# Attention, rational MLP and soft mixture of experts in one launch: accumulating DMAs started later, a conversion split between engines, more buffers for expert weights and a new table of priorities

## The chip, the cores and the metric

One core of a Trainium2 chip runs the whole program in one launch. The metric is the device time of that launch in microseconds (us). The core has TensorE (PE), VectorE (DVE), ScalarE (ACT), GpSimd (POOL) and SyncE (SP, which only issues DMAs here); 16 DMA engines are shared by all queues.

## The reference, cut to what matters

The three stages follow each other; `x` has 4608 rows of 512. Eight batches of 576 rows make up the 4608.

```python
k_p = k.reshape(B, H, Sp, pool, D).mean(axis=3)      # pool = 8, Sp = 72
v_p = v.reshape(B, H, Sp, pool, D).mean(axis=3)
attn = softmax(scale * q @ k_p.T);  x = attn @ v_p   # 8 heads of 64, to (4608, 512)

h = x @ w_in                                         # (4608, 2048)
P = a[0] + a[1]*h + a[2]*h*h + a[3]*h*h*h
Q = 1.0 + abs(b[0])*abs(h) + abs(b[1])*h*h
x = (P / (Q + 1e-6)) @ w_out                         # (4608, 512)

logits = x @ phi                                     # 32 slots: 8 experts of 4
d = softmax(logits, axis=0);  slot_input = d.T @ x
slot_out[e] = relu(slot_input[e] @ w1[e]) @ w2[e]    # each expert: 512 -> 1024 -> 512
out = softmax(logits, axis=1) @ slot_out
```

`w_in` and `w_out` arrive as 64-bit floats; all the rest is 32-bit.

## The kernel before, in words

The rows are cut into 36 tiles of 128, and the tiles into nine **runs** of four (`NR` = 9). `w_out` is never multiplied with the rows: it is folded into the router (`wpt`) and applied to the 32 slots at the end, so only the activation `A` of the MLP is kept.

- **Attention** (`attention(t)`, lines 410 to 490), one tile: scores `sc`, maximum, exponential, sum, normalisation, transposes `pt`, products `av`, and the split of the result into a rounded part `xh` and a rest `xl`. The tiles of run 0 come first; those of run r+1 are computed while run r is in its dense part.
- **Dense** (`dense(r, p)`), eight pairs of 128 columns a run: 24 products a pair into the buffer `h` (lines 558 to 560, two `h` buffers of two PSUM banks), then ACT (`s`, `a`, `u`), POOL (lines 577, 583, 585) and DVE (lines 580, 592, 594, 596) compute the rational function into `A`; `lg` (line 606) are the logits, line 617 transposes `A` into `G`. A new pair's products wait until line 580 has read the `h` that they overwrite.
- **Routing** (`routing(r)`) after a run: the maximum of the slots, the exponential `L`, its transposes `ptq` and `ptr`, a copy `en`, 128 products `pss` that sum `A` by slots, and their addition to the running sum `Sacc` (line 709).
- **Weights** (`win`, `wout`, `words`): each of 32 blocks of 512 KB is loaded as two 32-bit words per number and put together: one ACT operation on the high word (line 501), three DVE operations (lines 502, 504, 506). `win` then splits into `wh` (ACT 515, POOL 516), `wout` makes a column of `wpt` (products `wot`, `pw`).
- **Pooled keys and values**: batch 0 is reduced on DVE, the others by DMAs that add in DRAM (`summed`): one plain copy on SP, then seven accumulating DMAs on the POOL queue, each of which waits for the one before to land. Batch 1 has its own pair (`kr`, `vr`, 144 KB each DMA), batches 2 to 7 share one (`ksum`, `vsum`, 864 KB each).
- **Experts and tail**: `experts()` loads 8 blocks of `w_out` and 64 of `w1` and `w2`, 512 KB each, into whatever buffer has become free; `tail()` finishes the slots (`stp`, `slin`, `pi`), multiplies with `w1` (`l`) and `w2` (`lo`), and writes 18 blocks of the output.
- 120 idle products (line 327, each two records in the trace) fill PE's gaps before the first dense product.

The order on every engine is made when the program is built, by `Plan.run()`: a list scheduler with a duration for every operation. It takes the operation that could start first and, among equals, the one with the smallest key. A row of constants (`HEAD`, `FIRST`, `RUN`, `K_...`) gives the keys; they name times but only rank. Some operations carry an alternative on another engine (`alt`), allowed in run 0 and in the last run from pair `EITHER` on. Engines then execute that order strictly.

Of the kernel before, what the change touches and what calls it, by code (L numbers as in the profile page):

```python
# [10 lines left out]
I32 = mybir.dt.int32  # L11
AF = mybir.ActivationFunctionType
# [6 lines left out]
SP = 72  # L19
NT = B * S  # L20
DM = 512
# [9 lines left out]
HEAD, FIRST, RUN = 27.2, 101.2, 69.79  # L31
ATT, ATO = 18.86, -18.84
# [5 lines left out]
FINE, EITHER = 2, 6  # L38
LGN, LGL = 1, 7
RW, GD, AD = 2, 6, 0  # L40
A1, A1S = 23.71, 10.22
K_AS, K_A1, K_W, K_UW, K_LN, K_EX, K_U, K_A, K_LG, K_T, K_GT = 2.1, 7.21, -0.59, 8.21, 10.79, 0.89, 16, 0.1, 5.04, 27.99, 27.09
K_S, K_S1, K_S2, AXR = -14.78, 117.23, 23.77, 3
K_R, K_P1, K_P, K_IN, K_OUT, K_AT = 12.5, 13.81, 61.38, -40, -14.54, 1.58
# [78 lines left out]
class Task:  # L123
    __slots__ = ("alts", "key", "deps", "outs", "bufs", "n", "end", "start", "idx", "nbytes", "ready", "kind", "name")


class Plan:
# [46 lines left out]
    def run(self):  # L174
# [6 lines left out]
        for t in self.tasks:  # L181
            t.ready = 0.0
# [6 lines left out]
        while left:  # L189
# [16 lines left out]
            for t in live:  # L206
                s0 = t.ready
                if best and round(max(s0, min(free[a[0]] for a in t.alts)), 3) > best[0][0]:
                    continue
# [14 lines left out]
                for i, (e, d, fn, p) in enumerate(t.alts):  # L224
# [5 lines left out]
                    k = (round(s, 3), t.key, s + d, t.idx)  # L230
# [35 lines left out]
def soft_moe_kernel(ctx: ExitStack, tc: tile.TileContext, qT, kT, vP, kS, vS, kR, vR, w_in, w_out, ab, phi, w1, w2, sel, pick, out):  # L266
# [37 lines left out]
    vp = [fixed([SP, DM], f"vp{i}", np_=4) for i in range(2)]  # L304
# [11 lines left out]
    idle = buf("lg", [128, 128], "idle")  # L316
    lgb = buf("lg", [128, 2, 130], "lg", np_=2)
# [8 lines left out]
    for _ in range(FILL):  # L326
        op("PE", 0.22, lambda: p_.matmul(idle.t, ident, ident, start=True, stop=True), [idb], [idle], 1e6)
# [6 lines left out]
    run_len = lambda r: FIRST if r == 0 else RUN  # L334
# [24 lines left out]
    def summed(src, shape, name, key, step):  # L359

        d = fixed(shape, name, pool_=dr)
        n = 4 * shape[0] * shape[1]
        op("SP", 0.06, lambda: nc.sync.dma_start(out=d.t, in_=src[0]), [], [d], key, nbytes=2 * n)
        for w in range(1, 8):
            op("POOL", 1.0, lambda w=w: g_.dma_start(out=d.t, in_=src[w], accum_op=ALU.add, max_dma_last_dim=4 * shape[1]), [], [d], key + step * w, nbytes=3 * n)
        return d
# [3 lines left out]
    def pooling(b):  # L370
        need = att_key(first_tile[b])
        kb, vb = kp[b % 2], vp[b % 2]
        if b > 0:
            g, i, n = (0, 0, 1) if b == 1 else (1, b - 2, B - 2)
# [8 lines left out]
            op("SP", 0.06, lambda: nc.sync.dma_start(out=vb.t, in_=at_(1, SP)), [pooled[g][1]], [vb], key, nbytes=SP * 2048)  # L383
# [12 lines left out]
        for i in range(4):  # L396
# [4 lines left out]
            op("DVE", 1.2, lambda t=t, o=o, i=i: v_.tensor_reduce(out=o.t[:, 128 * i : 128 * i + 128], in_=t.t, axis=AX.X, op=ALU.add),  # L401
               [], [t, (o, i)], key, alt=[("POOL", 2.5, lambda t=t, o=o, i=i: tree(t.t, o.t[:, 128 * i : 128 * i + 128]), True)] if E0 & 8 else ())
# [3 lines left out]
    def attention(t):  # L406
# [87 lines left out]
    def words(src, t, key):  # L494
# [152 lines left out]
    def routing(r):  # L647
# [39 lines left out]
        for q in range(4):  # L687
# [11 lines left out]
            if q == 0:  # L699
                pssed[r] = P.tasks[-1]  # L700
# [314 lines left out]
```

## Time and profile before

| | |
|---|---|
| time, median of 3 runs | 868.07 us (867.98 to 869.91) |
| profiled execution | 867.88 us, of it 866.1 us span from first to last instruction |
| PE, DVE, ACT, POOL busy | 775.3, 665.6, 568.6, 500.6 us |
| first dense product of run 0, of run 1 | at 61.1 and 185.1 us |
| maximum of the slots (line 660) of run 1, 7, 8 | at 289.4, 706.8 and 766.1 us |
| mean granted clock of TensorE | 0.945 of full speed |

Two kinds of rows are read below: busy times by stretch, with the granted clock (1.00 is 2.4 GHz, 0.50 is 1.2 GHz) and the busy share of the DMA engines; and single waits, where the text behind `<-` names what ended them.

### The profile page before, as it was taken

To read this page: it belongs to the slowest core of one execution; us is meant where nothing else is said; L and a number is where in the kernel's file an instruction comes from. 1 tells how busy PE (TensorE), PEld (TensorE's weight loads), DVE (VectorE), ACT (ScalarE), POOL (GpSimd) and SP (SyncE) were. 2 spreads that over 40 slices of the span, in tenths; PEclk is the share of its full clock that TensorE was granted. 3 is DMA by queue.
4 is the path that set the end of the run, shared out by engine and by line. 5 is a ranking of instruction groups with operands and counts; after the bars stand their busy time and mean duration, and the time that the engine had idled before them with its cause. 6 is when DMAs were issued, how large, how long until landed. Compare 5 with 4: busy or idle time off the path is not lost.

```text
span 866.1 us, 15758 instructions
## 1 busy us (share of the span) xinstructions
PE 775.3 (90%) x6250; PEld 567.0 (65%) x6250; DVE 665.6 (77%) x977; ACT 568.6 (66%) x960; POOL 500.6 (58%) x304
## 2 busy tenths in 40 slices
PE   9889876999899999999999999999999988559992
PEld 9767655676777677677777768767767756324320
DVE  5757989774899898889998988989888888861011
ACT  2356856657678778968868877877896773721032
POOL 2524546146778767867858858876886875800000
PEclk9959968989999999999999999999999999969997
DMA  9997367972400000000000000000000643549959
GB/s 325 257 318 220 112 169 187 181 163 49 93 25 20 20 26 20 20 25 13 20 20 13 26 17 20 15 12 26 13 14 26 218 123 90 195 135 411 409 209 350
DMA packets 34709, 99.70 MB, mean 115 GB/s; under 512 B 4052, under 2 KB 5204, under 8 KB 34572
## 3 DMA queue, kind: packets, MB, share of 16 engines
q1 hardware_dynamic: 31724, 84.25, 27.9%
q0 software_dynamic: 2912, 14.45, 9.3%
q8 instruction: 49, 0.80, 0.4%
q14 instruction: 24, 0.20, 0.1%
HBM read 85.05 MB, written 30.15 MB: 133 GB/s over the span
## 4 chain that ended last, share of the span: by engine, by line
PE 61%; DVE 13%; ACT 12%; POOL 6%; DMA 4%; issue 2%; SPq 0%; ACTq 0%; DVEq 0%; POOLq 0%
PE h L558 13%; PE h L560 11%; PE h L559 11%; POOL a L577 5%; PE av L483 4%; DVE a L580 3%; PE sc L426 3%; PE pt L472 3%; PE lo L873 3%; PE lg L606 3%; ACT s L572 3%; DMA G<-in_w_out 2%; PE pw L537 2%; PE pss L694 2%; PE l L844 2%
## 5 line engine op out<-in xcount | busy, mean ns | idle before, releaser
L558 PE MATMUL h<-xh,wh 128*128 128x512 f32 x576 | 246.8, 428 | 19.0 <-DVE a L580 10.7
L560 PE MATMUL h<-xh,wh 128*128 128x512 f32 x576 | 230.9, 401 | 2.4 <-POOL wh L516 2.3
L559 PE MATMUL h<-xl,wh 128*128 128x512 f32 x576 | 230.3, 400 | 0.0
L577 POOL TENSOR_TENSOR a<-a,s 128x1024 f32<-128x1024 f32 (+1 forms) x66 | 154.3, 2338 | 86.7 <-ACT s L572 56.4
L585 POOL TENSOR_TENSOR u<-u,s 128x1024 f32<-128x1024 f32 (+1 forms) x72 | 168.2, 2338 | 5.6
L558 PEld LDWEIGHTS h<-xh,wh 128*128 128x128 f32 x576 | 110.6, 192 | 56.4 <-DVE a L580 15.5
L560 PEld LDWEIGHTS h<-xh,wh 128*128 128x128 f32 x576 | 110.5, 192 | 29.4 <-POOL wh L516 3.2
L559 PEld LDWEIGHTS h<-xl,wh 128*128 128x128 f32 x576 | 111.0, 193 | 19.5 <-DVE xl L488 0.4
L592 DVE SCALAR_TENSOR_TENSOR u<-u,r 128x512 f32<-128x512 f32 x144 | 96.5, 673 | 31.3 <-ACT r L591 30.9
L580 DVE SCALAR_TENSOR_TENSOR a<-h,abt,a 128x1024 f32<-128x1024 f32 (+1 forms) x74 | 92.6, 1251 | 33.2 <-POOL a L577 29.0
L574 ACT ACTIVATE a<-h,abt 128x1024 f32<-128x1024 f32 (+1 forms) x71 | 84.9, 1196 | 39.0 <-PE h L560 39.0
L591 ACT ACTIVATE r<-s 128x512 f32<-128x512 f32 x144 | 86.8, 604 | 30.6 <-DVE a L596 28.5
L594 DVE SCALAR_TENSOR_TENSOR r<-a,abt,r 128x512 f32<-128x512 f32 x144 | 106.0, 739 | 0.0
L583 POOL TENSOR_SCALAR s<-u,gb 128x1024 f32<-128x1024 f32 (+1 forms) x72 | 88.6, 1230 | 25.5 <-DVE a L577 14.2
L596 DVE SCALAR_TENSOR_TENSOR a<-u,r 128x512 f32<-128x512 f32 x144 | 97.5, 680 | 3.0
L588 ACT ACTIVATE s<-u,cc 128x1024 f32<-128x1024 f32 (+1 forms) x74 | 83.6, 1129 | 8.6 <-POOL u L585 6.2
L572 ACT ACTIVATE s<-h 128x1024 f32<-128x1024 f32 (+1 forms) x74 | 73.8, 998 | 21.4 <-PE h L560 18.4
L617 DVE STREAM_TRANSPOSE G<-a 128x1024 f32<-128x1024 f32 x64 | 79.0, 1237 | 1.0
L463 POOL TENSOR_TENSOR at<-at,st 128x576 f32<-128x576 f32 x35 | 40.6, 1161 | 66.8 <-PE av L483 26.5
L576 ACT ACTIVATE u<-h 128x1024 f32<-128x1024 f32 (+1 forms) x74 | 74.2, 1002 | 3.5 <-PE h L560 2.1
L475 ACT ACTIVATE a<-pt 72x512 f32<-72x512 f32 x72 | 40.8, 588 | 31.4 <-PE pt L472 31.1
L606 PE MATMUL lg<-a,wpt 128*32 128x128 f32 x1152 | 48.7, 285 | 12.6 <-DVE a L596 12.6
(165 smaller groups left out, 1060.0 us busy)
## 6 DMA issues: line engine op xcount, KB each, us to landing
wx<-in_w SPq DMA_DIRECT2D x46, 512.0 KB, 6.8
qt<-in_qT SPq DMA_DIRECT2D x35, 256.0 KB, 2.7
G<-in_w SPq DMA_DIRECT2D x16, 512.0 KB, 8.5
out_dram<-o SPq DMA_DIRECT2D x15, 512.0 KB, 5.3
G<-in_w_out SPq DMA_DIRECT2D x14, 512.0 KB, 5.0
ksum<-in_kS POOLq DMA_DIRECT2D x7, 864.0 KB, 8.9
vsum<-in_vS POOLq DMA_DIRECT2D x7, 864.0 KB, 8.7
G<-in_w_in SPq DMA_DIRECT2D x10, 512.0 KB, 6.8
```

Source lines behind the costliest of these rows:

```text
L558: p_.matmul(o, w[:, 0, k], xh[r].t[:, k], start=(k == 0), stop=False)
L559: p_.matmul(o, w[:, 0, k], xl[r].t[:, k], start=False, stop=False)
L560: p_.matmul(o, w[:, 1, k], xh[r].t[:, k], start=False, stop=(k == 3))
L572: op("ACT", t_act(n), lambda fl=fl: a_.activation(out=fl(S_), in_=fl(h), func=AF.Square), [pt_(h)], [pt_(S_)], c, after=was("sq"), also=[A ...
L577: mul = lambda eng, fl=fl: eng.tensor_tensor(out=fl(A), in0=fl(A), in1=fl(S_), op=ALU.mult)
L580: op("DVE", t_dve(n, 1), lambda fl=fl: v_.scalar_tensor_tensor(out=fl(A), in0=fl(h), scalar=a1, in1=fl(A), op0=ALU.mult, op1=ALU.add), [pt ...
L583: op("POOL", t_pool1(n), lambda fl=fl: g_.tensor_scalar(out=fl(S_), in0=fl(U), scalar1=gb.t[:, 1:2], scalar2=gb.t[:, 0:1], op0=ALU.mult, o ...
L585: mul = lambda eng, fl=fl: eng.tensor_tensor(out=fl(U), in0=fl(U), in1=fl(S_), op=ALU.mult)
L591: op("ACT", t_act(512, 0), lambda f=f, q=q: a_.activation(out=q.t, in_=S_.t[:, f], func=AF.Exp, scale=-1.0), [(S_, f)], [q], c + K_EX)
L592: op("DVE", t_dve(512), lambda f=f, q=q: v_.scalar_tensor_tensor(out=U.t[:, f], in0=U.t[:, f], scalar=QC, in1=q.t, op0=ALU.add, op1=ALU.mult),
L594: op("DVE", t_dve(512, 1), lambda f=f, q=q: v_.scalar_tensor_tensor(out=q.t, in0=A.t[:, f], scalar=a0, in1=q.t, op0=ALU.add, op1=ALU.mult) ...
L596: op("DVE", t_dve(512), lambda f=f, q=q: v_.scalar_tensor_tensor(out=A.t[:, f], in0=U.t[:, f], scalar=-2.0, in1=q.t, op0=ALU.add, op1=ALU. ...
```

## The change

- `summed` takes a time `at` before which none of its DMAs may be planned: 32 for batch 1, 95 for batches 2 and 3 and 168 for 4 to 7. The two sums of six batches are now a pair for two (288 KB each DMA) and a pair for four (576 KB): 42 accumulating DMAs in place of 28, of the same bytes in all.
- In `words`, ACT turns the low word into three bits (new operation), and DVE needs two operations in place of three, for all 32 blocks.
- `experts` may also use the three `S` buffers, `kp`, `vp` and `en`. On SP, 34 loads of 512 KB and a half one now stand behind the last run's `pss` products; before, 40.
- 30 idle products `spare` in the tail, which hold an `h` buffer until the last of them.
- The last run's `pss` are not added to `Sacc`, but copied and brought into `stp` by products of their own; its maximum and `lg` have their own bank; two operations of the tail are cut in halves.
- `EITHER` goes from 6 to 0: in the last run every pair may use the alternatives. All keys change.

```diff
-HEAD, FIRST, RUN = 27.2, 101.2, 69.79
+HEAD, FIRST, RUN = 36.72, 100.7, 66.96
...
-FINE, EITHER = 2, 6
+FINE, EITHER = 2, 0
...
-    def summed(src, shape, name, key, step):
+    def summed(src, shape, name, at):
...
-            op("POOL", 1.0, lambda w=w: g_.dma_start(out=d.t, in_=src[w], accum_op=ALU.add, ...), [], [d], key + step * w, nbytes=3 * n)
+            op("POOL", 1.0, lambda w=w: g_.dma_start(out=d.t, in_=src[w], accum_op=ALU.add, ...), [], [d], at, nbytes=4 * n, at=at)
...
+        if onact:
+            op("ACT", 0.63, lambda: a_.activation(out=raw.t[:, :, 0], in_=raw.t[:, :, 0].bitcast(U32), func=AF.Copy, scale=0.999 * 2.0**-29, bias=-0.4925), [], [raw], key)
+            op("DVE", 0.69, lambda: v_.scalar_tensor_tensor(out=ti(), in0=ti(), scalar=3, in1=raw.t[:, :, 0], op0=ALU.logical_shift_left, op1=ALU.bitwise_or), ...)
+            op("DVE", 0.69, lambda: v_.scalar_tensor_tensor(out=ti(), in0=raw.t[:, :, 1], scalar=-0x80000000, in1=ti(), op0=ALU.bitwise_and, op1=ALU.bitwise_or), ...)
+            return
...
+        if r == NR - 1:
+            lastp.append((ph, pk))
+            return
...
+        pairs = {28: ("q", "q"), 29: ("q", "at"), 30: ("at", "kp0"), 31: ("kp1", "vp0"), 32: ("vp1", "en")}
...
-                b = buf(["kv", "att"] if n < 6 else ["w", "gt", "A", "kv", "att"], [128, 2, 512], "wx")
+                b = buf(["kv", "att"] if n < 6 else ["w", "gt", "A", "S", "kv", "att"], [128, 2, 512], "wx")
...
+        spare = buf("h", [128, 2, 512], "spare")
+        prev = last_of["g1"]
+        for i in range(NFT):
+            prev = [op("PE", 0.22, lambda: p_.matmul(spare.t[:, 0, 0:128], ident, ident, start=True, stop=True), [idb], [spare], 1e6, after=prev)]
...
+        op("PE", 1.4, lambda: stp(pa, lambda b, n: Sacc.t[:, b, n, :], olds), [Sacc, olds], [pa], k0 - 1)
+        op("PE", 1.4, lambda: stp(pt, lambda b, n: cp[b // 2].t[:, b % 2, 32 * n : 32 * n + 32], self_), cp + [self_], [pt], k0)
+        op("DVE", 0.69, lambda: v_.tensor_tensor(out=sT.t, in0=pt.t, in1=sA.t, op=ALU.add), [pt, sA], [sT], k0)
```

POOL's queue in the head, before: from its first weight block on (`wh` is line 516 of a block, `at` the normalisation of an attention tile).

```order
L516 TENSOR_TENSOR wh<-wi,wh 128x512
L365 DMA kr<-in_kR 32x1152
L365 DMA vr<-in_vR 32x1152
L516 TENSOR_TENSOR wh<-wi,wh 128x512
L365 DMA ksum<-in_kS 144x1536
L463 TENSOR_TENSOR at_66<-at_66,st 128x8x72
L365 DMA vsum<-in_vS 144x1536
L516 TENSOR_TENSOR wh<-wi,wh 128x512 x2
L463 TENSOR_TENSOR at_66<-at_66,st 128x8x72
```

The same queue now, from the fourth weight block on; the first accumulating DMA comes behind five blocks and three normalisations.

```order
L530 TENSOR_TENSOR wh<-wi,wh 128x512
L470 TENSOR_TENSOR at_67<-at_67,st 128x8x72
L530 TENSOR_TENSOR wh<-G,wh 128x512
L372 DMA kr<-in_kR 32x1152
L372 DMA vr<-in_vR 32x1152
L530 TENSOR_TENSOR wh<-wi,wh 128x512
L372 DMA kr<-in_kR 32x1152 x2
L372 DMA vr<-in_vR 32x1152
L530 TENSOR_TENSOR wh<-wi,wh 128x512
```

All accumulating DMAs have moved behind the head's last normalisation, and those of one sum stand closer together than before.

PE around the sums of a steady run (run 4's, in run 5), before: nothing stands between the transposes `ptr` and the products `pss` that need their copy.

```order
L677 MATMUL ptq<-ident,L 128x128
L472 MATMUL pt<-ident,at_66 72x128 x4
L674 MATMUL ptr<-ident,L 128x128 x4
L694 MATMUL pss<-G,en 32x512 x64
L606 MATMUL lg<-a,wpt 32x128 x8
```

The same place now.

```order
L688 MATMUL ptr<-ident,L 128x128 x4
L572 MATMUL h<-xh,wh 128x512
L573 MATMUL h<-xl,wh 128x512
L574 MATMUL h<-xh,wh 128x512
...
L479 MATMUL pt<-ident,at_66 72x128 x4
L620 MATMUL bank<-a,wpt 32x128 x8
L708 MATMUL pss<-G,en 32x512 x64
```

Six dense products, four transposes and the logits of a pair (`bank`) now stand between them; the other steady runs read alike.

PE in the tail now, from the last run's sums on; before, the same rows without `spare` and with one `stp` of 64.

```order
L688 MATMUL ptr<-ident,L 128x128 x4
L793 MATMUL bank<-ident,m 1x128
L708 MATMUL pss<-G,en 32x512 x64
L798 MATMUL bank<-ident,mrow 128x1
L948 MATMUL pct<-ident,cTs 128x128 x4
L789 MATMUL spare<-ident 128x128 x2
L948 MATMUL pct<-ident,cTs 128x128 x4
L789 MATMUL spare<-ident 128x128 x5
L819 MATMUL stp<-self,cp 32x32 x64
L819 MATMUL stp<-olds,Sacc 32x32 x64
```

All 30 idle products stand behind `pss`, none ahead of it.

## Rows read from the trace of the kernel before

**Rows 1.** Busy time by stretch: the stages, all engines, clock, DMA share, GB/s

```profile
core 0: us, PE busy (x) PEld busy (x) DVE busy (x) ACT busy (x) POOL busy (x), PEclk, DMA share, GB/s
0.00:61.10 61.10, 52.92 (x393) 48.83 (x393) 35.43 (x63) 24.01 (x43) 22.52 (x29) 0.84 0.98 312
61.10:185.00 123.90, 103.68 (x644) 80.66 (x645) 107.47 (x154) 80.57 (x130) 58.98 (x47) 0.87 0.69 169
185.00:289.40 104.40, 100.31 (x728) 77.14 (x728) 82.11 (x129) 78.61 (x128) 71.98 (x42) 0.99 0.27 60
289.40:706.80 417.40, 403.68 (x3466) 306.26 (x3466) 370.79 (x527) 331.11 (x571) 312.12 (x166) 1.00 0.11 33
706.80:766.10 59.30, 38.48 (x363) 25.09 (x361) 52.63 (x73) 32.81 (x52) 34.70 (x23) 0.87 0.43 138
766.10:866.10 100.00, 76.19 (x661) 28.99 (x661) 17.16 (x37) 21.45 (x38) 0.29 (x1) 0.88 0.82 315
```

**Rows 2.** Chain that ended last, 18 to 62 us: start, us, what

```profile
7.61 10.39 DMA G<-in_w_in
...
21.64 17.24 DMA G<-in_w_out
```

**Rows 3.** DMA queues, 20 to 40 us and 40 to 61 us: packets, MB, share

```profile
q0 software_dynamic: 395, 2.03, 51.5%
...
q0 software_dynamic: 259, 1.17, 27.6%
```

**Rows 4.** Busy time in the head, as Rows 1

```profile
0.00:41.10 41.10, 36.22 (x300) 35.62 (x300) 24.77 (x42) 13.41 (x24) 16.54 (x24) 1.00 0.96 291
41.10:61.10 20.00, 16.70 (x95) 13.20 (x93) 10.66 (x21) 10.60 (x20) 5.98 (x5) 0.50 1.03 355
```

**Rows 5.** PE timeline, 38 to 41 us: start, us, records, wait before it

```profile
40.15 0.63 PE L472 MATMUL pt<-ident,at 128*72 128x128 f32 x4 [3.51 <-ACT a L475]
```

**Rows 6.** Groups by line, shapes apart: busy us, mean ns | idle before

```profile
L501 ACT ACTIVATE wi<-G 128x512 f32<-128x512 f32 x9 | 6.0, 669 | 4.7 <-DMA G<-in_w_in 4.6
L577 DVE TENSOR_TENSOR a<-a,s 128x1024 f32<-128x1024 f32 x8 | 11.7, 1457 | 2.2 <-ACT a L574 2.2
L585 DVE TENSOR_TENSOR u<-u,s 128x1024 f32<-128x1024 f32 x2 | 2.4, 1213 | 0.0
L694 PE MATMUL pss<-G,en 32*32 32x512 f32 x1024 | 40.0, 641 | 9.7 <-ACT en L679 9.7
L575 DVE TENSOR_SCALAR a<-h,abt 128x1024 f32<-128x1024 f32 x2 | 2.7, 1345 | 1.6 <-PE h L560 1.6
```

**Rows 7.** PE timeline, 708 to 716 us and the tail, as Rows 5

```profile
710.67 4.46 PE L694 MATMUL pss<-G,en 32*32 32x512 f32 x128 [1.65 <-ACT en L679]
...
769.07 7.07 PE L694 MATMUL pss<-G,en 32*32 32x512 f32 x128 [0.69 <-ACT en L679]
...
788.67 8.80 PE L844 MATMUL l<-wx,sp 128*32 128x512 f32 x72 [0.32 <-DVE sp L813]
...
830.25 2.79 PE L873 MATMUL lo<-wx,hT 128*32 128x512 f32 x7
```

**Rows 8.** Around the last run's sums and behind them, as Rows 1

```profile
754.50:775.00 20.50, 10.04 (x143) 4.46 (x151) 14.96 (x28) 6.21 (x14) 3.81 (x4) 0.50 0.48 178
775.00:836.00 61.00, 54.51 (x497) 20.06 (x489) 7.58 (x16) 6.23 (x13) 0.29 (x1) 1.00 0.87 345
...
770.00:778.00 8.00, 6.75 (x133) 3.11 (x101) 2.14 (x4) 0.00 (x0) 0.29 (x1) 0.69 0.10 12
778.00:829.40 51.40, 47.88 (x442) 18.10 (x441) 5.29 (x13) 5.16 (x11) 0.00 (x0) 1.00 1.02 406
```

**Rows 9.** Line 502 on DVE alone, by stretch

```profile
61.10:185.00 123.90, 9.74 (x22) 0.87 0.69 169
```

**Rows 10.** DMAs of `kr`, then of `ksum`: us from issue to landing

```profile
DMA to landing us min/median/max: 3.2/4.4/9.4
...
DMA to landing us min/median/max: 2.1/8.3/11.0
```

More of the change, by code (lines that the diff above doesn't have):

```diff
@@ L123 @@
 class Task:
-    __slots__ = ("alts", "key", "deps", "outs", "bufs", "n", "end", "start", "idx", "nbytes", "ready", "kind", "name")
+    __slots__ = ("alts", "key", "deps", "outs", "bufs", "n", "end", "start", "idx", "nbytes", "ready", "kind", "at")
 class Plan:
@@ L207, in run @@
                 s0 = t.ready
-                if best and round(max(s0, min(free[a[0]] for a in t.alts)), 3) > best[0][0]:
+                if best and int(max(s0, min(free[a[0]] for a in t.alts)) * 1000 + 0.5) > best[0][0]:
                     continue
@@ L265, in soft_moe_kernel @@
 @with_exitstack
[L266 removed]
+def soft_moe_kernel(ctx: ExitStack, tc: tile.TileContext, qT, kT, vP, kS, vS, kU, vU, kR, vR, w_in, w_out, ab, phi, w1, w2, sel, pick, out):
     nc = tc.nc
@@ L492, in soft_moe_kernel, with words @@
     wh = {}
-    def words(src, t, key):
+    def words(src, t, key, onact):
         if not wide:
@@ L511, in win @@
         t = buf(["t", "gt"], [128, 512], "wi")
-        words(w_in[f], t, key)
+        words(w_in[f], t, key, f < UI)
         wh[f] = buf("w", [128, 2, 4, 128], "wh", F32R, 2)
@@ L521, in wout @@
         t = buf(["t", "gt"], [128, 512], "wo")
-        words(w_out[f], t, key)
+        words(w_out[f], t, key, f >= UO)
         op("SP", 0.06, lambda: nc.sync.dma_start(out=wod[f].t, in_=t.t), [t], [wod[f]], key, nbytes=128 * 2048)
@@ L713, in soft_moe_kernel @@
     last = run_at(NR - 1)
-    end = last + RUN + 25
+    end = last + RUNL + 25
     def experts():
@@ new lines, in tail @@
+        ph, pk = lastp[0]
+        cp = [buf("U", [128, 2, 512], "cp", np_=2) for _ in range(2)]
+        flat = lambda t: t if len(t.shape) == 2 else t.rearrange("p a b -> p (a b)")
+        for src, o, part in ((ph, lambda: flat(cp[0].t), cp[0]), (pk[0], lambda: cp[1].t[:, 0], (cp[1], 0)), (pk[1], lambda: cp[1].t[:, 1], (cp[1], 1))):
+            n = 1024 if src is ph else 512
+            op("ACT", t_act(n), lambda src=src, o=o: a_.activation(out=o(), in_=flat(src.t), func=AF.Copy), [src], [part], k0 - 2,
+               alt=[("DVE", t_dve(n), lambda src=src, o=o: v_.tensor_copy(o(), flat(src.t)), False)])
@@ L777, in tr, with stp @@
+        sT = buf("t", [128, NF, 32], "sT", np_=2)
+        def stp(pt, part, scale):
             for n in range(NF):
                 for b in range(4):
-                    p_.matmul(pt.t[32 * b : 32 * b + 32, n, :], Sacc.t[:, b, n, :], self_.t, start=True, stop=True)
-        op("PE", 2.4, tr, [Sacc, self_], [pt], k0)
-        sT = buf("S", [128, NF, 32], "sT")
-        op("DVE", 0.69, lambda: v_.tensor_copy(sT.t, pt.t), [pt], [sT], k0)
+                    p_.matmul(pt.t[32 * b : 32 * b + 32, n, :], part(b, n), scale.t, start=True, stop=True)
```

145 lines of the change are left out of this document (87 added, 58 removed).

## The prediction

> **What bounds the kernel now.** I read the busy times by stretch first, to divide the 866.1 us into stages that have different limits [rows 1]. The head, up to the first dense product at 61.1 us, is a matter of DMA: the 16 engines are busy for 0.98 of it. Run 0, up to the first product of run 1 at 185, is crowded on DVE (107.5 of 123.9 us), with PE idle for 20.2 us. In the steady runs, up to 706.8, PE is the limit: 403.7 of 417.4 us, at full clock. The stretch up to 766.1 is DVE's again (52.6 of 59.3), and the last 100 us belong to DMA (0.82).
>
> Then the chain that ended last, in the head alone: 10.4 us of it wait for a block of `w_in`, 17.2 us for a block of `w_out` [rows 2]. What the engines carried meanwhile stands in the queue table: the accumulating DMAs (the software queue) took 51.5% of all DMA time from 20 to 40 us and 27.6% from 40 to 61 [rows 3], 16 us together, for sums that no engine reads before batches 1 and 2 are due. The wait reaches PE: 3.51 us of idling at 36.6 [rows 5], and then 20 us at the lower clock, 0.50 [rows 4].
>
> In the steady runs one wait repeats: `pss` waits for `en`, the copy of the transposes just before it, 9.7 us in eight runs [rows 6]. In the tail the timeline shows `pss` at 7.07 us where the run before took 4.46, because the clock is 0.50 [rows 7, 8]; DMA then lies idle (0.10) from 770 to 778 for want of free buffers, and from 778 to 829.4 it is full (1.02) [rows 8]. The products `lo` end 3.6 us behind it, at 833.0 [rows 7].
>
> **The change part by part.**
>
> *Accumulating DMAs later: the head.* None is left ahead of the last normalisation of the head on POOL. PE's own share of the head follows from the two halves [rows 4]: 36.2 us of work up to 41.1; behind it 16.7 us at half clock, which are 8.4 at full clock. Of the 4.9 us that PE is idle up to 41.1, the 3.5 for a block of `w_in` [rows 5] go and 1.4 stay. That is 46.0. The new order puts one more `wot` and `pw` ahead of the first dense product: six records, 1.0 us at the rate of the four in [rows 5]. The waits behind 41.1, 3.3 us, stay in the sum. It comes to 50.3, a gain of 10.8; I take **-10.5 us**. The bounds: -13.8 if these waits go too, since the 120 idle products stand in PE's queue and cannot be passed; 0 if the blocks come as late as now.
>
> *Low words on ACT.* Line 502 falls away: 9.74 us in 22 instructions of DVE between 61 and 185 [rows 9]. In the same stretch DVE gets two more multiplications of line 585 and one fewer of line 577: 2 x 1.21 less 1.46 [rows 6], 1.0 us. ACT gets 22 operations more; the nearest row is line 501, which also reads every second word, 669 ns [rows 6], so 14.7 us on top of 80.6 in 123.9 [rows 1]: 77%, with no engine fuller than DVE. What DVE gains can come back to PE only where PE waits: 20.2 us idle and, at a mean clock of 0.87 in that stretch, some 32 us at half clock, half of whose busy time is excess, 13 us; 4 us of idling stand between 185 and 289 [rows 1]. I take nine tenths of DVE's relief of 8.7 us, **-8 us**, because DVE is the fullest there. Bounds 0 (ACT in its place) and -20 (half of those 37 us).
>
> *New priorities, steady runs.* Six dense products, four transposes and a `lg` now fill the wait ahead of `pss`. Of the 9.7 us, 1.65 and 0.69 belong to the last two [rows 6, 7], so 7.4 lie in the steady stretch, 1.2 a run. The 192 dense products of a run share its 69.6 us (417.4 / 6) with all the rest, so six are worth 2.2 us at most; by two thirds of that, 1.4, they cover the wait alone. The `lg` there may itself wait for DVE, and I take **-6 us**. Bounds: -13.7, all of PE's idling [rows 1], and +5, half of it again.
>
> *Last run.* Before its `pss` only a `lg` stands in the 1.65 us, worth some 0.5 (eight records, by 128 in 4.46); two of the three operations of line 575 leave DVE, 2.7 us at 1.345 each [rows 6], and DVE is 89% busy. With `Sacc` written once less only behind the end of this stretch: **-3.5 us**, bounds -8 and +3.
>
> *Tail.* Loads behind `pss` fall from 40 to 34.5. Forty of 0.524 MB in 51.4 us are 408 GB/s; 5.5 fewer are **-7 us**. The loads that moved ahead find DMA idle (0.10, and 0.48 from 754.5) [rows 8]. PE allows it: the 256 products `l` and `lo`, at 8.80/72 us each [rows 7], last 31 us, from 788.7 to 820. The sums kept apart save additions to `Sacc` and cost a second group `stp` and a copy; both lie in the time in which DMA is full, and count nothing; without that cover they would be about even, some 2 us each way. `spare` holds one `h` buffer, so the second half of `l` waits for the first half's Relu, about 1 us, under the same cover. Bounds -9 and -2.
>
> *Idle products.* The clock was 0.50 from 754.5 to 775.0 and 1.00 from there to 836 [rows 8], and the order has all thirty behind `pss`. The Trainium skill, in TensorE: Matmul & The Clock Gate, section Part 1: The HAM clock gate, says that the throttled state is the default and that activity releases it; by that, products of no use ahead of `pss` would be worth 7.07 less 4.46, 2.6 us. By the order they stand where the rows show full clock already, so the sum has nothing for them; the page's rule would have made it 2.6 us shorter.
>
> The sum: -10.5 - 8 - 6 - 3.5 - 7 = -35 us. The profiled execution took 867.9 us, 0.2 under the median of 868.1, with 1.8 us outside its span; so **833 us**. No difference under 0.3% counts, since that is about what a measurement of this kernel can tell from no change.
>
> **The rivals.**
>
> *ACT takes DVE's place in run 0.* The earlier start is then handed back: run 1 begins no earlier, and the first two terms shrink from 18.5 to 2. For it: ACT also makes `xh`, `wt`, `wh` and the copies that PE waits for. Against: 77% against DVE's 87%. 867.9 - 18.5 = 849.
>
> *Run 0 closes up.* With both relieved, half of the 37 us goes, and the steady runs lose 10: -10.5 - 20 - 10 - 3.5 - 7 gives 817. For it: all three waits have the same root, one full engine. Against: DVE still has 80% there.
>
> *The new order opens waits in the steady runs.* All keys change, and PE stands still whenever line 580 is late; three more us in each of six runs turn -6 into +18, and the time into 857. Against: the key of line 580 goes down, so it is taken earlier.
>
> *POOL blocked by its own queue: slower.* An accumulating DMA waits in POOL's queue until the one before it has landed. `kr` took 4.4 us in the median and up to 9.4, `ksum` 8.3 [rows 10]. Between two of the same sum the order has at most one `wh`, one DMA of the other sum and itself, about 3 us by the 1.25 of a POOL instruction in the mean [rows 1], and once nothing. At 7 us of landing the six gaps of `kr` cost 24 us, and those of the next sum, of 288 KB between the two sizes, as much: 48 us on POOL, which makes `wh` for PE. If all of it reached PE: 833 + 48 = 881. It decides from 35 us on. Against: POOL is busy only 59 of 123.9 us [rows 1]. The Trainium skill, in DMA: Bandwidth & Descriptors, section Anatomy of one DMA, gives about 2.0 us and the bytes at 436 GB/s for such a DMA; by that a 288 KB one lands in 2.7 us, as an estimate, and the gaps would cost nothing. The rows disagree: even 144 KB took 4.4.
>
> **How the numbers follow.** The forecast (823 to 843) gets 0.52, ACT in DVE's place 0.15, run 0 closed up 0.17, new waits 0.08, POOL 0.06, and no change 0.02. Faster takes the first four less a hundredth of the fourth, 0.91; no change 0.03; slower 0.06. The range runs from 812, which leaves out the far side of the second rival, to 858, which leaves out POOL and part of the new waits: some 0.18 together.
>
> **What would show it.** The first dense product at 47 to 53 us, and no software queue above 10% before 40. The maximum of the slots of run 1 at 268 to 274, of run 8 near 738. No wait for `en` over 0.7 us in the steady runs. The last load landing 47 us behind `pss` instead of 53; `pss` still near 7 us. The forecast is wrong if ACT stands above 85% in run 0, if POOL waits for landings by more than 20 us, or if PE is idle by more than 25 us in the six steady runs.

## The result and the profile after

The changed kernel took 837.55 us (median of 4 runs, 835.03 to 840.35) against 868.79 us before: a ratio of 0.964 (95% interval 0.9607 to 0.9674), 31 us less. The forecast was 833, in a range of 812 to 858. The total came out nearly as forecast, the stages did not: run 0 gave far more than its term, and the steady runs and the tail gave nothing.

Busy time by stretch of the changed kernel, with the same columns and the same marks as [rows 1] (first dense product of run 0, of run 1; maximum of the slots of runs 1, 7 and 8):

```profile
core 0: us, PE busy (x) PEld busy (x) DVE busy (x) ACT busy (x) POOL busy (x), PEclk, DMA share, GB/s
0.00:50.20 50.20, 46.49 (x404) 44.51 (x405) 34.01 (x56) 30.18 (x56) 18.51 (x24) 1.00 0.88 292
50.20:156.30 106.10, 92.31 (x591) 75.34 (x590) 88.75 (x119) 84.71 (x142) 51.96 (x45) 0.89 0.67 170
156.30:261.60 105.30, 101.75 (x765) 77.69 (x763) 89.99 (x140) 83.53 (x136) 86.19 (x56) 0.97 0.59 114
261.60:681.00 419.40, 408.86 (x3479) 309.61 (x3478) 377.24 (x530) 335.01 (x572) 320.50 (x174) 1.00 0.14 41
681.00:735.10 54.10, 37.81 (x357) 24.20 (x357) 48.58 (x71) 36.85 (x56) 28.97 (x18) 0.83 0.51 172
735.10:835.60 100.50, 75.87 (x851) 37.53 (x851) 15.50 (x36) 22.64 (x41) 0.29 (x1) 0.86 0.77 285
```

Stage by stage against [rows 1], with the term of the sum behind it:

| stage | before | after | moved | forecast |
|---|---|---|---|---|
| head | 61.1 | 50.2 | -10.9 | -10.5 |
| run 0 | 123.9 | 106.1 | -17.8 | -8 |
| run 1 and six steady runs | 104.4 + 417.4 | 105.3 + 419.4 | +2.9 | -6 |
| last run | 59.3 | 54.1 | -5.2 | -3.5 |
| tail | 100.0 | 100.5 | +0.5 | -7 |

The head is now PE's own work (46.5 of 50.2 us), at full clock throughout. In the steady runs the wait for `en` of [rows 6] is gone, as forecast, but PE is hardly sooner done. The maxima that bound this stage moved with their keys, so the starts of the runs measure it better: from the first product of run 2 to that of run 8 it takes 418.6 us, before 419.2, while run 1, from its first product to that of run 2, takes 78.4 us, before 75.0. What PE waited for from 261.6 to 681 (total us, times, longest):

```profile
PE h L572 <- DVE a L594: 6.2, 7, 1.9
PE h L572 <- DVE Sacc L726: 1.1, 2, 0.6
PE pt L479 <- DVE Sacc L726: 0.6, 2, 0.3
PE bank L620 <- DVE a L610: 0.6, 2, 0.4
```

In the tail there is a wait that [rows 7] did not have. PE timeline behind the last run's `pss` (start, us, what; in brackets the idle time before it):

```profile
746.77 1.30 PE L819 MATMUL stp<-self,cp 128*32 128x32 f32 x128
747.91 0.47 PE L819 MATMUL stp<-olds,Sacc 128*32 128x32 f32 x34
753.11 1.50 PE L819 MATMUL stp<-olds,Sacc 128*32 128x32 f32 x94 [4.72 <-issue]
...
754.99 2.05 PE L789 MATMUL spare<-ident 128*128 128x128 f32 x8
...
757.05 1.38 PE L789 MATMUL spare<-ident 128*128 128x128 f32 x6
758.36 1.92 PE L834 MATMUL slin<-wx,sT 128*32 128x512 f32 x16
```

In the middle of the second group of `stp` PE stands still for 4.72 us, and the profile shows nothing that it waits for ("issue"). Then `slin` stands behind fourteen records of idle products; its operand `sT` was ready at 756.1. So `l` begins 26.7 us behind the first `pss`, where before it was 19.6. The loads notice it. DMA share behind `pss`, second last column:

```profile
744.00:756.50 12.50, 7.78 (x289) 7.47 (x290) 2.31 (x9) 3.17 (x6) 0.00 (x0) 0.79 0.93 349
756.50:761.00 4.50, 4.50 (x38) 2.58 (x41) 0.00 (x0) 0.28 (x1) 0.00 (x0) 0.81 0.09 33
761.00:774.00 13.00, 13.00 (x118) 7.32 (x110) 1.34 (x3) 1.47 (x4) 0.00 (x0) 1.00 0.92 302
774.00:797.00 23.00, 23.00 (x188) 8.95 (x187) 2.08 (x3) 1.53 (x3) 0.00 (x0) 1.00 1.03 411
```

From 756.5 to 761 DMA is idle (0.09): the next loads want buffers that `slin` still reads. The waits of the load queue show it (SP, total us, times, longest):

```profile
SPq L779 <- PE slin L834: 11.8, 2, 11.6
```

PE then works without a break from 764.8 to the last `lo` at 802.2. The last packet of the loads ends at 799.8, 56 us behind the end of `pss`, where the prediction had 47; before it was 54.5. It is the loads that set the end: in thirteen of the fourteen profiles read here the last `lo` ends 2.4 us behind the last load, and the kernel some 33 us behind that. The exception is stp_early.

### The profile page after: what moved, and what is told of

It reads as the page before. It is cut to its first block, busy times and chain, and to the rows that moved or that the text cites. A ratio compares the mean times of both kernels' runs of the same rounds, so it can differ in the third digit from the quotient of the medians.

```text
span 835.6 us, 16096 instructions
## 1 busy us (share of the span) xinstructions
PE 763.1 (91%) x6440; PEld 568.9 (68%) x6440; DVE 654.1 (78%) x946; ACT 592.9 (71%) x997; POOL 506.4 (61%) x317
## 4 chain that ended last, share of the span: by engine, by line
PE 66%; ACT 12%; DVE 11%; issue 3%; DMA 3%; POOL 3%; SPq 0%; ACTq 0%; DVEq 0%; POOLq 0%
PE h L572 14%; PE h L574 13%; PE h L573 13%; PE av L490 4%; PE sc L433 4%; PE pt L479 3%; PE bank L620 3%; PE lo L918 2%; ACT s L586 2%; ACT u L590 2%; DVE a L594 2%; POOL a L591 2%; PE l L889 2%; ACT a L588 2%; PE pss L708 2%
## 5 line engine op out<-in xcount | busy, mean ns | idle before, releaser
L572 PE MATMUL h<-xh,wh 128*128 128x512 f32 x576 | 242.9, 422 | 12.1 <-DVE a L594 9.3
L574 PE MATMUL h<-xh,wh 128*128 128x512 f32 x576 | 228.0, 396 | 0.0
L573 PE MATMUL h<-xl,wh 128*128 128x512 f32 x576 | 227.9, 396 | 0.0
L591 POOL TENSOR_TENSOR a<-a,s 128x1024 f32<-128x1024 f32 (+1 forms) x67 | 157.4, 2350 | 72.9 <-ACT a L588 56.1
L599 POOL TENSOR_TENSOR u<-u,s 128x1024 f32<-128x1024 f32 (+1 forms) x70 | 164.2, 2346 | 13.3 <-ACT s L596 5.7
L572 PEld LDWEIGHTS h<-xh,wh 128*128 128x128 f32 x576 | 109.1, 189 | 48.9 <-DVE a L594 12.2
L574 PEld LDWEIGHTS h<-xh,wh 128*128 128x128 f32 x576 | 109.0, 189 | 25.7
L608 DVE SCALAR_TENSOR_TENSOR r<-a,abt,r 128x512 f32<-128x512 f32 x144 | 106.6, 744 | 0.0
L597 POOL TENSOR_SCALAR s<-u,gb 128x1024 f32<-128x1024 f32 (+1 forms) x67 | 84.5, 1261 | 11.2 <-DVE a L591 6.2
L588 ACT ACTIVATE a<-h,abt 128x1024 f32<-128x1024 f32 (+1 forms) x73 | 86.9, 1190 | 3.8 <-PE h L574 3.8
L470 POOL TENSOR_TENSOR at<-at,st 128x576 f32<-128x576 f32 x35 | 42.7, 1219 | 49.9 <-DVE st L464 48.6
L620 PE MATMUL bank<-a,wpt 128*32 128x128 f32 x1152 | 49.9, 288 | 12.1 <-DVE a L610 12.1
```

What stands on the lines that cost most here:

```text
L572: p_.matmul(o, w[:, 0, k], xh[r].t[:, k], start=(k == 0), stop=False)
L573: p_.matmul(o, w[:, 0, k], xl[r].t[:, k], start=False, stop=False)
L574: p_.matmul(o, w[:, 1, k], xh[r].t[:, k], start=False, stop=(k == 3))
L588: op("ACT", t_act(n, 1, 2), lambda fl=fl: a_.activation(out=fl(A), in_=fl(h), func=AF.Identity, scale=a3, bias=a2), [pt_(h), abt], [pt_(A) ...
L591: mul = lambda eng, fl=fl: eng.tensor_tensor(out=fl(A), in0=fl(A), in1=fl(S_), op=ALU.mult)
L599: mul = lambda eng, fl=fl: eng.tensor_tensor(out=fl(U), in0=fl(U), in1=fl(S_), op=ALU.mult)
```

## The experiments

All were timed beside the kernel before, which took 866.8 to 869.5 us. Where orders are said to be kept, every engine's queue is that of the changed kernel but for the rows named. Eight of the kernels (the changed one among them) have the same order up to the last run; in their profiles run 1 begins anywhere from 155.0 to 160.2 us. So the head varies by itself, run 0 too (105.2 to 109.1 us in the eight), and tails are compared from the first `pss` of the last run to the end. Six kernels have the changed kernel's tail; in their profiles it takes 95.7 to 98.4 us, so a difference of under 3 us between two tails says little. Stages are read from one profile of each kernel, times from at least four runs.

**early_dma.** The accumulating DMAs return to POOL's first weight blocks (all 42; the sums stay cut in three). The numbers count the computing instructions of POOL ahead of each:

```diff
+early = {"kr": [1, 6, 11, 18, 21, 21, 22], "vr": [1, 6, 11, 18, 21, 22, 22],
+         "ks": [2, 9, 28, 31, 33, 37, 41], "vs": [3, 10, 28, 32, 35, 37, 47]}
```

> The changed kernel with the order of PE, DVE and ACT and of POOL's other instructions word for word as it is; only the accumulating DMAs go back to the places in POOL's queue that they had before the change (between the head's first weight blocks), and their first plain copies to the place in SP's queue. Theory of the prediction: the accumulating DMAs held up the weight blocks of the head and nothing later gives this back; the first dense product moves from 50.2 to about 60, run 1 starts near 166 in place of 156.3, and the time is about 848 us. Rival 1, run 0 is full and swallows the delay: the first dense product at about 60 all the same, but run 1 within 3 us of 156.3, time 837 to 841. Rival 2, the head is shorter by its new order alone: the first dense product stays within 2 us of 50.2, time 836 to 840.

857.55 us, ratio 0.989 (0.9857 to 0.9922): 20 us lost. The software queue's share of DMA time from 20 to 40 us, which the changed kernel doesn't have, and then the busy times of the rest of the head and of run 0:

```profile
q0 software_dynamic: 337, 1.26, 31.5%
```

```profile
41.10:64.60 23.50, 19.22 (x149) 16.74 (x148) 12.66 (x21) 15.01 (x29) 10.27 (x10) 0.79 0.78 251
64.60:175.40 110.80, 95.25 (x590) 77.27 (x590) 88.22 (x120) 84.46 (x141) 53.67 (x48) 0.87 0.70 178
```

The first dense product comes at 64.6 in place of 50.2, run 1 at 175.4 in place of 156.3. Both rivals fall: with the orders of PE, DVE and ACT untouched the head is 14.4 us longer, and run 0 does not swallow it but adds 4.7 (1.7 to 5.6 against the eight). The part is worth about twice its term.

**dve_low.** The low words back on DVE, at the same places:

```diff
-op("ACT", ..., func=AF.Copy, scale=0.999 * 2.0**-29, bias=-0.4925)
-op("DVE", ..., scalar=3, in1=raw.t[:, :, 0], op0=ALU.logical_shift_left, op1=ALU.bitwise_or)
+v_.tensor_scalar(..., scalar1=3, scalar2=0x7FFFFFFF, op0=ALU.logical_shift_left, op1=ALU.bitwise_and)
+v_.scalar_tensor_tensor(..., scalar=29, op0=ALU.logical_shift_right, op1=ALU.bitwise_or)
```

> The changed kernel with the order as it is, but the low words back on DVE: ACT's operation on them is left out, and at the place of the first of DVE's two operations stand the two of before, 32 times. Theory of the prediction (DVE sets run 0, relief of DVE comes back to PE by nine tenths): DVE gets some 0.4 us more for each of the 32 blocks, 13 us in all, of which about 8 lie behind the first dense product; run 1 starts about 8 us later, at 164, and the time is about 846 us. Rival, run 0 became shorter by its order, and DVE has room: run 1 within 3 us of 156.3, time 836 to 841.

847.05 us, ratio 0.975 (0.9713 to 0.9788): 9.5 us lost, and run 1 begins at 164.7, 4.5 to 9.7 us later than in the eight. Run 0:

```profile
51.60:164.70 113.10, 96.16 (x591) 78.32 (x590) 102.17 (x144) 74.48 (x120) 52.78 (x45) 0.86 0.63 160
```

DVE has 102.2 us of work in it in place of 88.8, and the run is 7.0 us longer (4.0 to 7.9 against the eight). The term of 8 us is about right.

**both_undone.** Both edits at once.

> The changed kernel with its orders, but with both parts undone that were undone singly: the accumulating DMAs at their early places, and the low words on DVE. Theory A (the two act in different places, the one on DMA and POOL's queue, the other on DVE): the losses add, 20 + 9.5, about 867 us; then all the rest of the change (priorities, buffers, idle products, sums apart) is worth next to nothing in sum. Theory B (both relieve the same full stretch, run 0, and either loss hides the other): 857 to 861, and the rest of the change is worth 8 us or more.

860.09 us, ratio 0.99 (0.9872 to 0.9928). The two losses do not add in the time (29.5 against 22.5), so theory B holds: they relieve partly the same stretch. The rest of the change is worth 8.7 us. None of that has come in when run 2 begins. Run 0 and run 1 of this kernel, and run 1 of the kernel before:

```profile
66.20:181.00 114.80, 96.97 (x590) 78.53 (x590) 98.70 (x139) 74.80 (x120) 53.70 (x47) 0.86 0.68 173
181.00:260.90 79.90, 76.42 (x564) 57.83 (x562) 64.58 (x102) 59.98 (x92) 57.73 (x37) 0.96 0.42 83
...
185.10:260.10 75.00, 70.91 (x497) 54.88 (x495) 54.37 (x88) 52.44 (x82) 48.27 (x30) 0.98 0.33 72
```

With DMAs and low words as before run 0 takes 114.8 us, 9.1 less than the 123.9 of [rows 1]; PE has 590 records in it and not 644, because the new order moves transposes and logits of run 0 behind the start of run 1. But run 1 is 4.9 us longer for it, and the head is 5.1 us longer (66.2 against 61.1): run 2 begins at 260.9, where before it began at 260.1. Up to there, without the two edits, the new order only moves time. What it gains comes later: 2.1 us from run 2 to run 8, 5.9 from the start of run 8 to the first `pss` (83.9 against 89.8), and 1.3 in the tail.

**only_late_dma.** The kernel before, with the earliest times alone.

```diff
-    def summed(src, shape, name, key, step):
+    def summed(src, shape, name, at):
...
-    pooled[1] = [summed(x, [144, 1536], n, K_S + K_S1, K_S2) for x, n in ((kS, "ksum"), (vS, "vsum"))]
+    pooled[1] = [summed(x, [144, 1536], n, 94.78) for x, n in ((kS, "ksum"), (vS, "vsum"))]
```

> The kernel before with one part of the change alone: the accumulating DMAs get the earliest times 32 and 95 (two sums as before, not three), all keys, the low words and the tail as before; the planner orders anew around them. Theory A (in the changed kernel their return cost 20 us, 14 in the head and 5 in run 0, so the part alone is worth about as much): the first dense product at 47 to 52, run 1 near 168, 850 to 856 us. Theory B (run 0 of before is full on DVE and hands back most of it): the first dense product at 47 to 52 too, run 1 not before 178, 861 to 867 us.

907.25 us, ratio 1.047 (1.0425 to 1.0514): outside both theories. The first dense product comes at 57.7, later than both theories said, and run 1 at 157.9, earlier than theory A said; but run 2 begins at 301.9, where before it was 260.1. The instructions on `ksum`, with first and last start:

```profile
L366 POOL DMA_DIRECT2D ksum<-in_kS x7: 862/871/901, 122.1 to 247.4; - x7
L379 SPq DMA_DIRECT2D ks<-ksum x6: 320/327/368, 254.8 to 460.9; - x6
```

The sum of all six batches is complete only behind 247.4, and batch 2 is loaded at 254.8. In the changed kernel the seven DMAs of the sum for two batches start from 106.8 to 161.8, and batch 2 is loaded at 166.2. So it seems to be the cut into a pair for two batches and a pair for four, on which the prediction had no term, that lets the sums start late at all; no run has the cut alone. How much of the early start of run 1 is moved work cannot be read from this run.

**kr_12.** One key of the steady runs' routing set back; the order behind it is planned anew.

```diff
-K_R, K_P1, K_P, K_IN, K_OUT, K_AT = 25, 5, 26.99, -39.28, -20, 1.63
+K_R, K_P1, K_P, K_IN, K_OUT, K_AT = 12.5, 5, 26.99, -39.28, -20, 1.63
```

> The changed kernel with one key set back, K_R (the rank of a steady run's maximum, exponential, transposes and sums) from 25 to the 12.5 of before; the planner then orders anew from run 1 on. Theory of the prediction (the dense products ahead of pss are worth 1.2 us a run): pss waits for en again, some 6 us in six runs, and the time is about 843. Rival (pss takes an h buffer, so it would have to wait for line 594 soon after anyway; of the 6.2 us of waits for en, 4 came back as waits for 594, 610 and 726): the waits change their names, and the time is within 2.5 us of 837.5.

844.66 us, ratio 0.9729 (0.9695 to 0.9763). The wait for `en` is back, in the same six runs as above:

```profile
PE h L572 <- DVE a L594: 7.1, 13, 0.8
PE pss L708 <- ACT en L693: 5.7, 5, 1.2
```

Of the 7 us, 3.3 stand in the steady runs: from the start of run 2 to that of run 7 it takes 355.4 us, the changed kernel 352.2, the kernel before 351.7. Another 3.7 are a later start of run 1, within the spread of the eight. So neither theory holds alone: the dense products ahead of `pss` are worth 0.7 us a run within the new order (theory: 1.2), and the rest of the new order costs as much again. The 352.2 of the changed kernel contain 1.6 us of a dip of the clock (last section), which kr_12 has not; without it the products are worth 1.0.

**no_extra_buffers.** The expert weights lose the buffers that the change gave them. With `pairs` empty they also lose the three `q` halves and the `at` half, which the kernel before had for two blocks: 42 loads stand behind the last run's `pss`, not 40 as expected.

```diff
-pairs = {28: ("q", "q"), 29: ("q", "at"), 30: ("at", "kp0"), 31: ("kp1", "vp0"), 32: ("vp1", "en")}
+pairs = {}
...
-b = buf(["kv", "att"] if n < 6 else ["w", "gt", "A", "S", "kv", "att"], ...)
+b = buf(["kv", "att"] if n < 6 else ["w", "gt", "A", "kv", "att"], ...)
```

> The changed kernel with the expert weights allowed only the buffers of before (no S, kp, vp, en, q and at halves): 40 loads behind the last run's pss in place of 34.5; order up to the tail as it is. Theory of the prediction (DMA sets the tail, 1.285 us for each load): 5.5 x 1.285 = 7.1 us slower, about 844.5. Rival (PE sets it: behind the gap among the stp, PE goes from l to the last lo, 764.8 to 802.2, without a wait, while the last load has landed near 797): the first 4 of the 7 us are hidden, about 841.

846.72 us, ratio 0.9756 (0.9722 to 0.979): 9.2 us lost. From the first `pss` to the end it takes 106.6 us in place of 97.5; DMA is full until 802, 68 us behind the first `pss` (1.03 and then 0.10):

```profile
770.00:802.00 32.00, 31.80 (x194) 10.96 (x193) 2.08 (x3) 1.64 (x3) 0.00 (x0) 1.00 1.03 410
802.00:812.00 10.00, 7.98 (x33) 2.72 (x34) 0.94 (x3) 0.97 (x3) 0.00 (x0) 1.00 0.10 41
```

The rival falls: these loads are not hidden behind PE. There are 7.5 more of them than in the changed kernel, so the 9.1 us are 1.2 us a load, near the 1.285 of the prediction.

**no_spare.** `NFT = 0`, no idle products in the tail.

> The changed kernel without the 30 idle products of the tail; all else in order, some of the tail's buffers fall otherwise. Theory A (products of no use stand in PE's queue ahead of slin and pi when these are ready): 2.3 us ahead of slin and 0.4 behind pi are given back, but the 4.7 us in which PE waits for nothing the profile shows between the two groups of stp stay, moved by some products at most: about 835 us. Theory B (they only fill waits): within 1 us of 837.5. Theory C (they keep the clock up, so they are worth something): 1 to 3 us slower.

836.42 us, ratio 0.9644 (0.9613 to 0.9674). The median cannot tell this from the changed kernel; the tail in the profile is 93.8 us in place of 97.5, and `l` begins 24.3 behind `pss`. The gap stands where it stood:

```profile
751.33 0.62 PE L819 MATMUL stp<-olds,Sacc 128*32 128x32 f32 x48
756.55 1.29 PE L819 MATMUL stp<-olds,Sacc 128*32 128x32 f32 x80 [4.60 <-issue]
```

**stp_early.** The group of the running sum, and the copy of its result, stand between the `pss` products.

```diff
-K_TL, K_RL, K_RP, K_F, RUNL = 18.94, -0.32, -27.03, -13.78, 51.58
+K_TL, K_RL, K_RP, K_F, RUNL = 18.94, -0.32, -27.03, -30, 51.58
...
-op("PE", 1.4, lambda: stp(pa, ...), [Sacc, olds], [pa], k0 - 1)
+op("PE", 1.4, lambda: stp(pa, ...), [Sacc, olds], [pa], k0 - 28)
```

> The changed kernel with three keys of the tail lowered, so that the products stp of the running sum, and what they need, stand between the last run's pss products, and not behind the stp of the last run's own sums. Theory F (256 short products in a row empty PE's instructions faster than they are fetched): the 4.72 us of idling with no releaser shrinks below 2 us, slin starts 6 to 8 us earlier behind pss, and with it l and the loads that wait for slin: 830 to 832 us. Rival (the gap comes from the loads that fill the DMA queues at that time, whatever PE runs): a gap of 4 to 5 us still stands behind pss, and only the 1.5 us of one stp group are gained: 835 to 837.

835.73 us, ratio 0.9638 (0.9606 to 0.9669): no gain that can be measured, though the gap among the `stp` is gone (1.42 us stand in `slin`) and `l` begins 22.3 us behind `pss`. The last `lo` ends as late as ever, 64.9 behind it, and 6.3 us behind the last load: in this kernel alone PE is behind the loads. Its last rows:

```profile
796.79 0.94 PE L789 MATMUL spare<-ident 128*128 128x128 f32 x6
797.65 1.90 PE L918 MATMUL lo<-wx,hT 128*32 128x512 f32 x4
799.49 0.94 PE L789 MATMUL spare<-ident 128*128 128x128 f32 x6
800.35 1.91 PE L918 MATMUL lo<-wx,hT 128*32 128x512 f32 x4
```

Idle products now stand between the last `lo`. Four records of `lo` take 1.90 us there, the last twelve 5.7 in three such groups. The 92 just before take 14.18 us, 0.62 for four; but the last ones are slower in any case, for in stp_early_no_spare, where nothing parts them, the last twelve take 4.4 us.

**stp_early_no_spare** and **stp_adjacent_no_spare.** The same without idle products; in the second, the key is `k0 - 20`, and the early group stands right behind `pss`.

> The changed kernel with the early stp group between the pss products and without the idle products. Theory F (the gap without a releaser came from 256 short products in a row, and the idle products cost PE 3 us by themselves and again between the last lo, where they keep neighbouring products from running side by side): the last lo ends 58 to 60 us behind the first pss in place of 64.1, and the time is 831 to 833. Rival (each of the two alone gained only 1 to 2 us because DMA is the limit behind them): 835 to 836.5.

> The same without idle products, but with the group stp of the running sum directly behind pss, so that the two groups are parted by four transposes only. Theory F: a gap of 3 to 5 us without a releaser stands in the second group or in slin, and the time is 2 to 4 us above that of stp_early_no_spare. Rival (the gap depended on the order of the groups or on a wait that the profile doesn't show): no gap above 1 us, and the time is 1 to 2 us below it, since pss ends 1.3 us earlier and the loads with it.

834.13 us, ratio 0.9593 (0.9564 to 0.9623), and 832.92 us, ratio 0.9569 (0.9538 to 0.96). The first falls between the ranges of its two theories, and only the second is clear of the changed kernel's interval. The first has no gap at all; the second has one in its second group, as theory F says, but half as long:

```profile
748.51 0.65 PE L819 MATMUL stp<-self,cp 128*32 128x32 f32 x50
751.50 0.96 PE L819 MATMUL stp<-self,cp 128*32 128x32 f32 x78 [2.34 <-issue]
```

It costs the second nothing: the last `lo` ends 59.6 and 59.5 us behind the first `pss`, with tails of 92.6 and 92.5 us. The loads set the end, and they start when `pss` ends, 1.2 us sooner in the second; the last one lands 48.3 and 49.5 us behind the end of `pss`.

**fill_before_sums.** All orders kept, 32 and 12 more idle products ahead of the last two groups of logits, writing a buffer of `pss`:

```diff
+p_.matmul(ph.t[:, 0, 0:128], ident, ident, start=True, stop=True)
```

> The changed kernel with all orders as they are, and 44 more idle products on PE, 32 ahead of the last but one group of logits of the last run and 12 ahead of the last one, where PE waited 7.1 and 3.6 us for DVE; they write a buffer of pss before pss starts. Theory R (the clock falls because PE idles there, and comes back only through work): the clock stays at 1.00 from 720 on; pss takes 4.5 us in place of 5.85, the two groups of logits 0.65 in place of 1.25 each, the transposes 0.5 less: 2.5 to 3.5 us faster, about 834.5. Theory N (the clock goes by something else, or the products are in the way of the logits): pss still 5.8 to 7, time 837 to 839.

840.13 us, ratio 0.9678 (0.9647 to 0.971). Nothing gained: the logits run at full clock, but the clock falls behind the next wait, and `pss` takes 5.89 us.

```profile
736.61 0.47 PE L693 MATMUL ptq<-ident,L 128*128 128x128 f32 x1 [2.03 <-DVE L L679]
...
739.49 5.89 PE L710 MATMUL pss<-G,en 32*32 32x512 f32 x128 [0.47 <-ACT en L695]
```

**adjacent_fill_to_sums.** stp_adjacent_no_spare with idle products in every wait up to `pss`: 30, 14, 8, 3 and 2.

> The kernel of stp_adjacent_no_spare with all its orders, and 57 idle products on PE in every wait from the last dense product to pss: 30 and 14 ahead of the last two groups of logits, 8 ahead of ptq, 3 ahead of ptr, 2 ahead of pss. In fill_before_sums the clock held to 735.8 and fell in the 2 us of waiting ahead of ptq, 3.7 us before pss. Theory R (work in every wait holds the clock; pss then takes 4.5 us in place of 5.9 and pss, which gates the loads, ends earlier): the clock stays at 1.00 from 720 to the end of pss, and the time is 1.5 to 3 us below stp_adjacent_no_spare, about 831 at 868.8 of before. Rival (the idle products delay the transposes, or the clock falls all the same): 833 to 836.

830.58 us, ratio 0.9552 (0.9525 to 0.958), the fastest of all. The granted clock is 1.00 from 692 to 750, and `pss` ends 4.80 us behind its start (5.85 in the changed kernel):

```profile
735.64 2.05 PE L1004 MATMUL pss<-ident 128*128 128x128 f32 x16
737.74 0.33 PE L693 MATMUL ptq<-ident,L 128*128 128x128 f32 x1
...
740.16 1.15 PE L710 MATMUL pss<-G,en 32*32 32x512 f32 x32
...
741.55 3.40 PE L710 MATMUL pss<-G,en 32*32 32x512 f32 x96
```

From the first `pss` to the end it is 88.8 us, 8.2 less than before the change. The time is 2.3 us below that of stp_adjacent_no_spare, but the intervals of the two ratios overlap.

## Why the prediction was right, and where it was not

- **Head, -10.5:** right in size (-10.9) and cause. PE's own work came to 46.5 us, the sum had 47.0. early_dma shows that the accumulating DMAs alone are worth 14.4 us there. The size is in part luck: without the two edits the new order makes the head 5.1 us longer (both_undone), and the sum had 1.0 for that.
- **Run 0, -8:** the mechanism was right, the term mis-sized; it measured -17.8. The low words are worth about the 8 us said of them, though by other factors: DVE is relieved of 13.4 us and half of it comes back, 7.0 (dve_low), in place of nine tenths of 8.7. Missing were the 4.7 us that the accumulating DMAs cost in run 0 (early_dma), which I had looked for in the head alone; together the two edits are worth 8.7 there (both_undone). The other 9.1 us the new order takes out of run 0 without either edit, but it puts 4.9 into run 1 and 5.1 into the head. By its size it is the rival "run 0 closes up", but the 10 us that this rival expected of the steady runs did not come. The rival "ACT takes DVE's place" falls: ACT is busy for 84.7 of 106.1 us, 80%.
- **Steady runs, -6:** wrong; +2.9 with run 1, and -0.6 from run 2 to run 8. "Six dense products, four transposes and a `lg` now fill the wait" was right: 7.4 us of waits for `en` became none. The failed step is to set the rest of the new order to nothing. PE now waits 2.3 us for `Sacc` and a logit's `A`; run 1 has transposes and logits of run 0 to do and is 3.4 us longer; and 3.4 us at half clock behind a wait for line 594 cost 1.6 (below). From run 2 to run 8 PE idles 2.6 us less than before and is busy 2.0 us longer. kr_12, planned anew, gives the products 0.7 us a run, 1.0 without the dip.
- **Last run, -3.5:** -5.2, within its bounds. It does not come from the DMAs or the low words, for both_undone has it too; which part of the new order brings it, no run separates.
- **Tail, -7:** wrong; +0.5. The loads are worth what was said: with 7.5 of them more the tail is 9.1 us longer, so the 5.5 of the change are worth some 6.7. The failed step is "both lie in the time in which DMA is full, and count nothing". The second `stp` group brought the gap of 4.72 us, and the idle products kept `slin` waiting. This delayed not only PE but the loads, which wait for the buffers that `slin` and `l` read, and so the end: the last load landed 56 us behind `pss`, with both mended 48 to 50, which is near the 47 of the prediction. Together the additions cost some 7 us (no_extra_buffers against before: 106.6 and 97.0, of which its two loads more are 2.4). With both mended the tail is 4.5 us shorter than before, with the clock held as well 8.2; the term was 7.
- **Idle products, nothing:** in the time these thirty cannot be told from nothing (no_spare is 1.1 us below the changed kernel), but they hold `slin` up by 2.2 us, and beside the mended `stp` the kernel without them has the shorter tail (92.6 against 99.5). In the prediction the rule that it names from the Trainium skill, in TensorE: Matmul & The Clock Gate, section Part 1: The HAM clock gate, would have given 2.6 us to products ahead of `pss`. adjacent_fill_to_sums against stp_adjacent_no_spare gives 2.3, not clear of noise in the time, but `pss` took 4.80 us at clock 1.00 in place of 7.61 at 0.58; and that only with work in every wait. With some of the waits filled it was nothing.
- **POOL blocked by its own queue:** up to 180 us POOL waited 19 us for landings of `kr` and `vr`, near the 20 at which the forecast would have been in doubt; run 0 was shorter all the same.

So the total was right in part because two errors cancelled: run 0 gave 9.8 us more than its term, the steady runs and the tail 16.4 less.

Three figures of the prediction do not follow from its own words: half of 37 us is 18.5 and not 20, half of 13.7 is 6.9 and not 5, and eight records by 128 in 4.46 are 0.3 us and not 0.5. None decides the forecast.

What the gap consists of is argued, not shown: the argument is that PE has no instructions left and waits for more. In its favour: where 256 `stp` follow each other it stands in every profile (4.50 to 5.75 us in eight kernels), with four transposes between the groups it is 2.34 and 2.02, and there is none in the kernel before with 128, nor in stp_early_no_spare, where `pss` products part the groups; stp_early has the 1.42 us in `slin`. During the gap one packet of 0.02 MB ran in the instruction queue, while DMA was full of expert loads:

```profile
q1 hardware_dynamic: 500, 1.81, 100.0%
q8 instruction: 1, 0.02, 1.2%
```

The Trainium skill, in Runtime: NRT & Kernel Launch, section Instruction fetch mechanics, says that instructions arrive in blocks of 16 KiB over DMA and that crossing a block's boundary is mostly hidden. The packet agrees with the size, 16384 bytes; the gap, if it is a fetch, was not hidden. One thing more speaks for it: in all eleven gaps, that of stp_early included, such a packet ends 1.3 to 1.5 us before PE goes on (751.72 and 753.11 in the changed kernel). Why the packet comes so late, no run shows.

## What to carry to other kernels

Ask of every DMA in a full stretch when its result is needed, and start it no earlier, but count how long the chain of sums takes from there: in smaller sums the late start gained 20 us, while the kernel before, with one large sum, lost some 40 by it. A run that becomes shorter may only have handed work to its neighbours: look at where the run after next begins. An added piece of work is covered only if nothing behind it frees the buffers on which the covering transfers wait. Idle products held the clock here only where they stood in every wait ahead of the work that needs it; behind it they held that work up.

## What was not expected of the hardware

- Behind a single wait of PE in a busy stretch the clock can fall. In steady run 4 PE waits 1.88 us, and the granted clock is 0.50 for the 3.4 us from 430.5; eight dense products take 0.43 us each in place of 0.23, 1.6 us in all. The dip stands in seven of the eight profiles with this order. In the eighth, no_extra_buffers, as in early_dma and both_undone, PE waits 1.86 us at the same place and the clock stays at 1.00, so the wait alone does not decide it. First the changed kernel, then no_extra_buffers:

```profile
427.90 0.64 PE L620 MATMUL bank<-a,wpt 128*32 128x128 f32 x16
430.42 0.74 PE L572 MATMUL h<-xh,wh 128*128 128x512 f32 x1 [1.88 <-DVE a L594]
430.96 0.63 PE L573 MATMUL h<-xl,wh 128*128 128x512 f32 x1
431.39 0.63 PE L574 MATMUL h<-xh,wh 128*128 128x512 f32 x1
...
427.95 0.51 PE L572 MATMUL h<-xh,wh 128*128 128x512 f32 x1 [1.86 <-DVE a L594]
428.29 0.39 PE L573 MATMUL h<-xl,wh 128*128 128x512 f32 x1
```

- PE can stand still for 4.7 us with nothing in the profile to wait for, where 256 very short products follow each other while DMA is full, and goes on 1.4 us behind the end of an instruction packet.
- Products of 32 columns of the array are dearer where products of the whole array part them: the last twelve `lo` take 5.7 us in three parted groups (stp_early) and 4.4 in a row (stp_early_no_spare), in another order among themselves.
